# Three places instead of four for streamed weight blocks, one more block kept in SBUF

## Chip, cores, metric

One core of a Trainium2 chip. The metric is the device time of one execution in microseconds, as a median over runs; lower is better. In the texts and profile lines PE is the TensorE matmul engine (PEld its weight loads), DVE, ACT and POOL are VectorE, ScalarE and GpSimd, and SP is the engine whose queue issues the loads; SBUF and PSUM are the memories on the core.

## The reference, cut to what matters

The program does two independent things and joins the results: a state-space convolution B (2048 positions, 1024 channels), and a recurrent attention A in which each of 64 segments needs the memory rows that the segment before it has put out.

```python
for s in range(n_seg):                      # 64 segments of 32 rows, in series
    xs = x[:, s * seg_len:(s + 1) * seg_len, :].copy()
    h = jnp.concatenate([mem, xs], axis=1)
    q = jnp.einsum('btd,dhe->bhte', h, Wq)  # 1024 x 4096 each, bf16
    k = jnp.einsum('btd,dhe->bhte', h, Wk)
    v = jnp.einsum('btd,dhe->bhte', h, Wv)
    # ... masked softmax over 40 keys ...
    o = jnp.einsum('bhtk,bhke->bhte', p, v)
    o = jnp.einsum('bhte,hed->btd', o, Wo)  # 4096 x 1024
    mem = o[:, :M, :].copy()                # 8 rows for the next segment
```

(The index letters of the third product are shortened.) The weights are 64 blocks of 128 x 2048 bf16, 512 KB each, 32 MB together. They do not all fit into SBUF, and each segment needs all of them.

## The kernel before

Part B comes first and also prepares what part A needs: the streamed weight blocks are copied into DRAM tiles of their own (`WD`). Then the loop over the segments runs. A block is resident in SBUF, or kept in PSUM (two blocks), or streamed into one of four places, in turn:

```python
STREAM = {("k", 0): (0, 5), ("q", 0): (3,), ("k", 1): (0, 3), ("q", 1): (0, 4), ("v", 0): (0, 4), ("v", 1): (0, 4)}
STREAM_O = (0, 4, 8, 11, 13)
# ...
SLOTS = 4
# ...
    def unit(key):
        if key in rest:                       # first segment: a resident block comes in
            rest.remove(key)
            load_resident(tc, wres, src, key, W_res)
        if key in W_res:
            return W_res[key]
        if key in kept:
            return ahead_of.pop(key)
        between.pop(key, lambda: None)()      # small transfers hung in between
        t_ = wst.tile([128, 2048], BF16, name="wst", tag="w%d" % (loads[0] % SLOTS))
        loads[0] += 1
        nc.sync.dma_start(out=t_[:], in_=WD[key][:])
        return t_
# ...
            for kc in kcs:                    # one projection, 8 blocks
                w = unit((m, t, kc))
                for g in range(4):
                    for o_, rhs in columns(w, 512 * g, 512):
                        nc.tensor.matmul(a[32 * g:32 * g + 32, o_:o_ + rhs.shape[1]], lhsT=hT[:, kc, :], rhs=rhs,
                                         # ...
```

The place of a block is free again when PE has done its 4 matmuls (8 in the output product). SP then issues the next load into it; SP takes its instructions in program order. In part B, sums over residue classes of the input u ("class sums") run in the gaps of a loop of 17 rounds of 8 steps:

```python
            if e % 2 == 0 or (e == 7 and sb % 4 == 1):
                step_side()
```

## Time and profile before

| | before |
|---|---|
| median, 4 runs (2662.08 to 2674.72) | 2667.72 us |
| first segment's output in the profiled run | 925.0 us |
| distance of two segments' outputs, mean of 63 | 26.49 us |
| PE's waits for streamed blocks per segment | 3.46 us |
| DMA share and rate in the loop | 0.95, 335 GB/s |
| issue of a streamed load to its last engine's landing, median of 970 | 5.59 us |

The segment distance times 63 is 1669 of the 2655 us in the profile: a tenth of a microsecond per segment is 6.3 us. A place goes through a turn: PE frees it, SP issues, the load lands, PE uses it. With four places, the load of a streamed block cannot be issued before PE has finished the streamed block four earlier. The profile lines for these numbers stand in the prediction.

### The profile page before, as it was taken

To read this page: it belongs to the slowest core of one execution; us is meant where nothing else is said; L and a number is where in the kernel's file an instruction comes from. 1 tells how busy PE (TensorE), PEld (TensorE's weight loads), DVE (VectorE), ACT (ScalarE), POOL (GpSimd) and SP (SyncE) were. 2 spreads that over 40 slices of the span, in tenths; PEclk is the share of its full clock that TensorE was granted. 3 is DMA by queue.
4 is the path that set the end of the run, shared out by engine and by line. 5 is a ranking of instruction groups with operands and counts; after the bars stand their busy time and mean duration, and the time that the engine had idled before them with its cause. 6 is when DMAs were issued, how large, how long until landed. Compare 5 with 4: busy or idle time off the path is not lost.

```text
span 2655.4 us, 76588 instructions
## 1 busy us (share of the span) xinstructions
PE 2099.2 (79%) x32856; PEld 1120.4 (42%) x32902; DVE 1498.8 (56%) x3224; ACT 1022.6 (39%) x1550; POOL 311.7 (12%) x601
## 2 busy tenths in 40 slices
PE   1688788675978588888887887788888888888878
PEld 1365555532433244444444444444444444444444
DVE  9677777879882254445454545454545454454440
ACT  6888888831212132323232222222322323232221
POOL 2133433540001000000000000000000000000020
PEclk6799999888999698999999999999999999998899
DMA  5665854742339999999999999999999999999992
GB/s 138 173 192 161 247 165 137 189 125 87 116 127 333 334 335 328 330 349 329 344 334 347 339 334 322 332 331 335 340 332 339 339 337 338 344 332 321 317 352 88
DMA packets 373171, 729.62 MB, mean 275 GB/s; under 512 B 117654, under 2 KB 209782, under 8 KB 370782
## 3 DMA queue, kind: packets, MB, share of 16 engines
q1 hardware_dynamic: 354942, 671.08, 74.4%
q0 software_dynamic: 14128, 39.99, 4.4%
q10 hardware_dynamic: 3760, 13.65, 1.4%
q8 instruction: 257, 4.21, 0.6%
q14 instruction: 84, 0.69, 0.1%
HBM read 669.80 MB, written 67.36 MB: 278 GB/s over the span
## 4 chain that ended last, share of the span: by engine, by line
DMA 39%; PE 31%; DVE 10%; issue 8%; ACT 7%; POOL 1%; SPq 0%; ACTq 0%; POOLq 0%; DVEq 0%
PE acc L329 16%; DMA wst<-WD_o 16%; DMA wst<-WD_v 11%; DMA wst<-WD_k 7%; PE pp L428 3%; PE pe L551 2%; ACT sn L1019 2%; DMA wst<-WD_q 2%; PE pro L151 2%; ACT kM L994 1%; PE tr L340 1%; ACT E L991 1%; PE ups L850 1%; PE pro L138 1%; DVE nr L995 1%
## 5 line engine op out<-in xcount | busy, mean ns | idle before, releaser
L329 PEld LDWEIGHTS <-hT 128*32 128x32 bf16 x12352 | 344.8, 101 | 464.9 <-issue 222.2
L329 PE MATMUL acc<-wst,hT 128*32 128x512 bf16 x2816 | 302.3, 413 | 138.0 <-DMA wst<-WD_v 57.0
L335 ACT CAST ev<-acc 128x512 bf16<-128x512 f32 x384 | 224.8, 585 | 432.7 <-PE acc L329 428.3
L428 PEld LDWEIGHTS <-oT 128*32 128x32 bf16 x8192 | 209.7, 98 | 209.5 <-issue 182.4
L329 PE MATMUL acc<-W_q,hT 128*32 128x512 bf16 x3328 | 240.2, 394 | 0.0
L329 PE MATMUL acc<-W_k,hT 128*32 128x512 bf16 x2816 | 238.2, 442 | 0.0
L428 PE MATMUL pp<-wst,oT 128*32 128x256 bf16 x2560 | 132.7, 284 | 128.2 <-DMA wst<-WD_o 119.8
L268 DVE TENSOR_SCALAR piece<-keep 128x256 int32<-128x256 int32 (+1 forms) x640 | 189.3, 361 | 78.4 <-PE pp L428 58.2
L428 PE MATMUL pp<-W_o,oT 128*32 128x256 bf16 x5120 | 217.3, 280 | 6.6 <-DMA W_o<-in_A_Wo_dram 6.6
L329 PE MATMUL acc<-W_v,hT 128*32 128x512 bf16 x3072 | 216.0, 384 | 8.2 <-DMA W_v<-in_A_Wv_dram 8.2
L367 DVE TENSOR_REDUCE mx<-sc 128x8 f32<-128x320 f32 x128 | 62.6, 489 | 219.5 <-PE sc L360 219.4
L341 DVE COPY KT<-tr 128x512 bf16<-128x512 bf16 x64 | 27.1, 424 | 267.1 <-PE tr L340 267.1
L415 ACT CAST oT<-pv 128x512 bf16<-128x512 f32 x128 | 74.9, 585 | 195.5 <-PE pv L401 194.3
L1158 PE MATMUL yp<-Bt,mi 128*128 128x512 bf16 x379 | 112.8, 403 | 39.8 <-DMA mi<-MId 30.4
L348 POOL COPY KT<-pk 128x128 bf16<-128x128 bf16 x128 | 37.7, 294 | 882.9 <-PE acc L329 545.3
L341 ACT COPY QT<-tr 128x512 bf16<-128x512 bf16 x128 | 74.9, 585 | 166.3 <-PE tr L340 165.4
L518 ACT CAST ob<-pp 128x128 bf16<-128x128 f32 x64 | 17.0, 265 | 291.2 <-DVE ob L517 291.2
L995 DVE SCALAR_TENSOR_TENSOR nr<-kM,ptt 128x656 f32<-128x656 f32 x128 | 104.8, 831 | 42.8 <-ACT kM L994 42.6
L151 PE MATMUL pro<-xTl,wsl 128*128 128x512 bf16 x493 | 116.5, 384 | 13.0 <-DVE kst L155 7.7
L517 DVE CAST ob<-pp 128x128 bf16<-128x128 f32 x64 | 18.6, 291 | 181.4 <-PE pp L428 181.4
L302 POOL COPY hT<-xt 128x192 bf16<-128x192 bf16 x64 | 22.2, 347 | 760.2 <-DMA xt<-XTd 632.3
L369 ACT ACTIVATE sc<-sc 128x320 f32<-128x320 f32 x128 | 54.0, 422 | 147.5 <-DVE sc L368 143.6
(284 smaller groups left out, 3820.2 us busy)
## 6 DMA issues: line engine op xcount, KB each, us to landing
wst<-WD_o SPq DMA_DIRECT2D x320, 512.0 KB, 9.7
wst<-WD_k SPq DMA_DIRECT2D x256, 512.0 KB
wst<-WD_v SPq DMA_DIRECT2D x256, 512.0 KB, 5.9
wst<-WD_q SPq DMA_DIRECT2D x192, 512.0 KB, 4.7
Ud<-ux POOLq DMA_DIRECT2D x16, 1024.0 KB, 4.7
uq<-Ud SPq DMA_DIRECT2D x32, 512.0 KB, 7.5
pk<-PKd SPq DMA_DIRECT2D x64, 192.0 KB, 5.0
wsl<-in_A_Wk_dram SPq DMA_DIRECT2D x16, 512.0 KB, 4.5
```

Of the source, the lines that this page charges most:

```text
L151: nc.tensor.matmul(a[:], lhsT=w[:, kc, 128 * j:128 * j + 128], rhs=xTl[:, kc, :, :].rearrange("p s k -> p (s k)"), start=(kc == 0), stop=( ...
L268: nc.vector.tensor_scalar(out=out.bitcast(I32), in0=in_.bitcast(I32), scalar1=0, scalar2=None, op0=ALU.bitwise_or)
L329: nc.tensor.matmul(a[32 * g:32 * g + 32, o_:o_ + rhs.shape[1]], lhsT=hT[:, kc, :], rhs=rhs, start=(kc == 0), stop=(kc == KC - 1), tile_pos ...
L335: nc.scalar.copy(out=q[:], in_=a[:])
L341: eng(out=dst, in_=p[:, i, :, :, :])
L367: nc.vector.tensor_reduce(out=mx[:], in_=sc, axis=AX.X, op=ALU.max)
L369: nc.scalar.activation(out=sc, in_=sc, func=ACT.Exp, scale=scale)
L415: nc.scalar.copy(out=o[:], in_=p[:].rearrange("p a (g q) -> p a g q", g=4))
L428: nc.tensor.matmul(po[32 * qt:32 * qt + 32, :], lhsT=oT[:, h % 4, (h % 16) // 4, :], rhs=columns(w, 1024 * hh + 256 * qt, 256)[0][1], star ...
L551: nc.tensor.matmul(pe[n][:], lhsT=left[2 * b + hi // 16][:, 128 * (hi % 16):128 * (hi % 16) + 128], rhs=wo[u][:, 1024 * hh + 512 * n:1024 ...
L995: v.scalar_tensor_tensor(out=nrs[e // 4][:, e % 4].rearrange("p f t j -> p f (t j)"), in0=kM[:], scalar=MAGIC, in1=ptv, op0=ALU.subtract, ...
L1158: pe.matmul(yp[:], lhsT=m_[:, cs, kc, :], rhs=Bt[:, kc, half, j, c_, :], start=(n == 0), stop=(n == 15))
```

## The change

Intent: 4 KB per partition of SBUF go from the fourth place to one more resident block, so that a sixteenth less is streamed. Besides, the class sums start two steps later and end in the last round.

```diff
-STREAM_O = (0, 4, 8, 11, 13)
+STREAM_O = (0, 4, 8, 11)
...
-SLOTS = 4
+SLOTS = 3
...
-            if e % 2 == 0 or (e == 7 and sb % 4 == 1):
+            if (e % 2 == 0 and (sb or e)) or sb == 16:
                 step_side()
```

## The prediction

> **What bounds the kernel now.** I read the page first (busy shares, the slices over time, the queues), then the table of windows over the second part, then the chain of waits there, the table of waits, and last the timeline block by block. The program has two parts. Up to about 800 us it builds a convolution; from 868 us to 2594 us it walks 64 segments in series (63 distances of 26.5 us from the first to the last output copy, 925.0 to 2594.2 us). Each segment multiplies by 64 weight blocks of 512 KB: 46 stay in SBUF, two stay in PSUM, 16 are streamed anew through four places. The second part is two thirds of the span, so it decides. The page, then the window over 63 segments (PE, PEld, DVE, ACT, POOL, granted clock, DMA share, GB/s):
>
> ```profile
> DMA  5665854742339999999999999999999999999992
> q1 hardware_dynamic: 354942, 671.08, 74.4%
> 925.00:2594.20 1669.20, 1375.03 (x26838) 715.36 (x26840) 819.54 (x2269) 486.63 (x945) 70.35 (x203) 0.94 0.95 335
> ```
>
> The DMA engines look full (0.95), PE is busy 82%. A reader would conclude "DMA-bound: one block of 16 less is a sixteenth of the loop". The chain of waits says otherwise (start, us, what):
>
> ```profile
> 1407.29 5.24 DMA wst<-WD_v
> 1412.53 0.04 issue
> 1412.57 1.05 PE acc L329 x16
> ...
> 1415.78 5.79 DMA wst<-WD_o
> 1421.57 0.04 issue
> 1421.61 0.92 PE pp L428 x24
> ...
> 1424.52 5.63 DMA wst<-WD_k
> ```
>
> It alternates. A DMA piece starts when PE has finished with a place and SP issues the next load into it, and ends when that load lands. Its 5 to 6 us are four transfers' time, because three others stand before it; then PE work follows, then another such turn. So the loop is bound by turns of places woven with PE work, not by either alone. The sizes, over those 63 segments (total, times, longest):
>
> ```profile
> PE pp L428 <- DMA wst<-WD_o: 117.2, 149, 2.7
> PE acc L329 <- DMA wst<-WD_v: 56.3, 72, 2.1
> PE acc L329 <- DMA wst<-WD_k: 36.9, 44, 1.8
> PE acc L329 <- DMA wst<-WD_q: 7.4, 17, 1.1
> ```
>
> Their sum is 217.8 us, 3.46 us per segment. PE work, with its small waits for other engines, is the other 23 us.
>
> **What the Trainium skill says.** "DMA: Bandwidth & Descriptors", section "Why a DMA increments its semaphore by 16 and not by 1": a load is spread over up to 16 engines which finish independently, and only the full count says it has landed. The trace agrees: over 970 streamed blocks the 16 updates of one semaphore lie 1.86 us apart from first to last (median), the last comes 1.18 us after the middle one, and issue to last update is 5.59 us. So a block waits for its unluckiest engine, and a short queue leaves the lucky ones idle. Same page, "Anatomy of one DMA": about 2 us fixed beside bytes/436e9, stated for the GpSimd path. For 512 KB that gives 3.2 us; the trace's fastest undisturbed 512 KB load, of the spectra, issued by SP, took
>
> ```profile
> DMA to landing us min/median/max: 3.7/7.5/9.6
> ```
>
> 3.7 us. "HBM Reference", "Specifications (TRN2)": a core streaming alone gets about 425 GB/s. Here a 4 KB packet usually takes 159 ns on its engine, which over 16 engines is 412 GB/s; the mean is 183 ns, as one packet in fourteen takes over 200 ns. So 335 GB/s holds much waiting, and a DMA share of 0.95 is not the ceiling it looks.
>
> **The change, part by part.**
>
> (a) *One block less.* Wo block 13 becomes resident. It is still multiplied, so PE work is unchanged. Its 8-matmul group at 0.4 us is no longer waited for. Transfer per segment falls from 16 blocks at 128 packets x 183 ns / 16 engines = 1.46 us by one. If transfer alone were the bound, this would save 63 x 1.46 = 92 us.
>
> (b) *Three places.* I took from the timeline, for 56 segments, the distance from one streamed block's first matmul to the next one's, less the waits for DMA. In order of use (us): k0 1.62, k5 1.77, q3 1.57, k1:0 0.74, k1:3 2.10, q1:0 0.90, q1:4 1.36, v0:0 1.34, v0:4 1.75, v1:0 1.55, v1:4 1.25, o0 1.04, o4 2.18, o8 0.80, o11 0.63, o13 2.32; sum 22.92. A turn of four places costs 5.59 us (issue to landing) plus 0.47 us (matmuls on the block, SP's issue) = 6.06 us and brings PE four blocks on. Where four distances sum to less, the turn is longer and PE waits for the excess. The best set of turns that do not overlap: k1:0 to v0:0 (0.74+2.10+0.90+1.36 = 5.10, excess 0.96), v0:0 to o0 (5.89, 0.17), o0 to o13 (1.04+2.18+0.80+0.63 = 4.65, 1.41). Sum 2.54, so 25.46 us per segment. Measured is 26.4: scatter of the landings adds 0.9, as the longest of several random sums exceeds the sum of means.
>
> The same with three places. A turn has one transfer less before it, 5.59 - 1.46 = 4.13, but cannot go far below the undisturbed 3.7 us, and the trace shows the floor coming: where the earlier load's middle engine finished 2.75 us after this issue, this one's did 1.50 us later; with 1.75 us it was 1.92, with 1.25 us 2.01. Engines ran dry between. I add 0.3 for that: 4.43 + 0.47 = 4.9 us (estimate). Now o11's distance is 0.63+2.32 = 2.95. The best set: k5 to k1:3 (1.77+1.57+0.74 = 4.08, excess 0.82), q1:0 to v0:4 (0.90+1.36+1.34 = 3.60, 1.30), v0:4 to o0 (4.55, 0.35), o0 to o11 (4.02, 0.88). Sum 3.35, so 26.27; with the same 0.9 of scatter 27.2. Against 26.4 that is +0.8 us per segment, 63 x 0.8 = +51 us. So the lost place should cost more than the lost block gives. The waits for DMA should grow from 3.5 to 4.3 us per segment, while the DMA share falls to about 0.87 (bytes per segment 335 x 26.5 = 8.88 MB, less 0.52 MB; 0.95 x 8.36/8.88 x 26.5/27.2).
>
> (c) *First segment and end.* Resident and streamed loads together stay 36 in the first segment: about +2 us for the shorter queue. The final product has one block less to fetch, behind ten resident ones: nothing.
>
> (d) *Class sums later.* The order of instructions shows the same counts on PE and the sums moved back. At the start two exponent groups now come before the first sum (1.7 us in the chain). By the end of round 15 the side work has taken 63 steps instead of 68, so five sums run in round 16. The first falls into this hole of PE and is free:
>
> ```profile
> 552.32 0.25 PE L899 MATMUL kp<-cs 128*64 128x41 bf16 x2 [9.16 <-DVE cs L1027]
> ```
>
> The other four stand between the last groups of kernel products: 4 x 1.05 = 4.2 us, on the chain that releases the next stage. In return five sums leave earlier rounds, where ACT, DVE and PE alternate on the chain: about 0.8 us each (my estimate: half of the 1.05 us on PE, as about every second sum is in the chain, and half of an evacuation of 0.6 us), 4 us. Sum: 4.2 - 4 - 1.7 = -1.5 us, rounded to -2.
>
> Total: 51 + 2 - 2 = +51; 2671 + 51 = 2722 us, taken as 2723.
>
> **The rivals.** *Transfer bound:* the share 0.95 speaks for it; 63 x 1.46 = 92 us come back, about 2580 us. Against it: waits for DMA are only 3.46 us per segment, so even their end would give PE's 22.9 us, and the chain is half PE. A milder form, in which the slow packets come on all engines at once, makes the queue's depth matter little: waits then fall by up to 1 us, 2610 to 2650. The spread of 1.86 us within a block speaks against that. *Floor of the turn higher than I took:* if a turn of three costs 4.6 + 0.47 = 5.07 us, each of the four turns loses 0.17 more than I took, 63 x 0.68 = 43 us: 2766 us. The bend from 1.50 to 2.01 us speaks for this. *A new wait elsewhere:* SP issues in order, and the next segment's small load xt is now issued one release later; POOL's copy of it ended at 1629.75 us where DVE began the pieces of block 15 at 1629.68, so about a microsecond could come on the path at the segment's end. But the queue before it is one block shorter. That would be up to +30 us.
>
> **Range and chances.** The turn's length decides: 4.82 us in place of 4.9 gives +0.5 per segment (2703), 5.07 gives +1.5 (2766). I allow for the milder rival below and the new wait above: 2660 to 2785. Slower by over 2% begins at 2724, right at my value: nearly even between same and slower. Faster needs under 2617, thus nearly the pure transfer bound: 6%.
>
> **What would show each step.** Segment distance 27.2 us; waits of PE for streamed blocks about 4.3 us per segment; DMA share about 0.87 with GB/s near 305; issue to landing in the chain 4 to 5 us instead of 5 to 6, with four turns per segment; the first part within 4 us of before. I am wrong if the share stays at 0.95 with shorter segments (transfer bound), if PE's waits for streamed blocks fall, or if the first part moves by more than 10 us.

## The result, and the profile after

2849.78 us (median of 4, 2829.47 to 2859.03) against 2667.72: 6.7% slower, ratio 1.0671 with a 95% interval of 1.0605 to 1.0737. A ratio in this document is the mean time of one kernel's runs over the mean of the other's in the same rounds, so not quite the ratio of the medians. The edit leaves every block multiplied from its own tile.

The window over the 63 segments of the changed kernel, with the same columns as in the prediction:

```profile
940.20:2796.80 1856.60, 1390.86 (x26838) 719.80 (x26840) 824.91 (x2269) 486.86 (x945) 70.32 (x203) 0.94 0.85 284
```

The stretch is 1856.6 us instead of 1669.2: 29.47 us per segment, 2.98 more. PE's busy time and the granted clock are nearly the same, and the DMA share fell from 0.95 to 0.85. So no engine got more work; all of them stand still more. The waits of PE in that stretch (total, times, longest):

```profile
PE acc L329 <- DMA wst<-WD_k: 136.5, 119, 3.1
PE pp L428 <- DMA wst<-WD_o: 135.3, 164, 2.4
PE acc L329 <- DMA wst<-WD_v: 95.3, 116, 3.2
PE acc L329 <- DMA wst<-WD_q: 30.0, 43, 2.7
```

They sum to 397.1 us, 6.30 us per segment instead of 3.46. That is 2.84 of the 2.98 us. The chain of waits shows what such a wait is now:

```profile
1234.44 0.84 PE pp L428 x24
...
1236.56 0.43 PE pp L428 x8
1237.01 5.16 DMA wst<-WD_k
1242.17 0.04 issue
1242.21 0.87 PE acc L329 x10
1243.09 4.47 DMA wst<-WD_k
1247.60 0.40 PE acc L329 x4
...
1250.14 4.58 DMA wst<-WD_v
1254.76 1.07 PE acc L329 x16
1255.91 0.59 ACT ev L335
1256.50 0.04 issue
1256.55 0.42 PE acc L329 x4
1256.99 4.85 DMA wst<-WD_o
```

Four turns of 4.5 to 5.2 us in 25 us, with some 6 us of other work between them. This is one of the quicker stretches: over the whole loop the chain holds 3.7 such pieces per segment, 5.27 us each in the mean; in the kernel before it holds 2.5, of 5.97 us. One load in four-place streaming took 5 to 6 us; a load with one transfer less before it should have been 1.46 us quicker, and it is only some 0.7 us quicker. Over 816 streamed loads of this trace the median from issue to last landing is 4.87 us.

The first segment's output comes at 940.2 us instead of 925.0, so 15 us of the 202 us between the two profiled runs arise before the second segment.

### The profile page after: what moved, and what is told of

The parts are those of the page before. It is cut to its first block, busy times and chain, and to the rows that moved or that the text cites. A ratio compares the mean times of both kernels' runs of the same rounds, so it can differ in the third digit from the quotient of the medians.

```text
span 2857.3 us, 76451 instructions
## 1 busy us (share of the span) xinstructions
PE 2117.5 (74%) x32856; PEld 1124.8 (39%) x32902; DVE 1498.7 (52%) x3224; ACT 1023.9 (36%) x1550; POOL 306.9 (11%) x601
## 4 chain that ended last, share of the span: by engine, by line
DMA 46%; PE 26%; issue 8%; DVE 8%; ACT 7%; POOL 1%; SPq 1%; ACTq 0%; POOLq 0%; DVEq 0%
DMA wst<-WD_k 15%; DMA wst<-WD_o 14%; PE acc L329 12%; DMA wst<-WD_v 12%; PE pp L428 4%; DMA wst<-WD_q 3%; ACT sn L1020 2%; PE pe L551 2%; PE pro L151 1%; PE ups L850 1%; DVE nr L995 1%; ACT E L991 1%; PE tr L340 1%; ACT kM L994 1%; DVE m L1109 1%
## 5 line engine op out<-in xcount | busy, mean ns | idle before, releaser
L329 PE MATMUL acc<-W_v,hT 128*32 128x512 bf16 x3072 | 223.4, 394 | 9.2 <-DMA W_v<-in_A_Wv_dram 9.2
L329 PE MATMUL acc<-W_k,hT 128*32 128x512 bf16 x2816 | 226.1, 424 | 0.0
L428 PE MATMUL pp<-wst,oT 128*32 128x256 bf16 x2048 | 106.1, 283 | 143.1 <-DMA wst<-WD_o 137.3
L341 DVE COPY KT<-tr 128x512 bf16<-128x512 bf16 x64 | 27.2, 425 | 253.2 <-PE tr L340 253.2
L1075 PE MATMUL hps<-KT,MF 128*128 128x512 bf16 x374 | 95.3, 401 | 17.8 <-DVE x L1088 13.4
L994 ACT ACTIVATE kM<-ptt,magic 128x656 f32<-128x656 f32 x128 | 103.8, 811 | 7.1 <-PE ptt L931 7.1
```

The source lines that it names most:

```text
L341: eng(out=dst, in_=p[:, i, :, :, :])
L428: nc.tensor.matmul(po[32 * qt:32 * qt + 32, :], lhsT=oT[:, h % 4, (h % 16) // 4, :], rhs=columns(w, 1024 * hh + 256 * qt, 256)[0][1], star ...
L994: sc.activation(out=kM[:], in_=ptv, func=ACT.Identity, bias=magic[:])
L1075: pe.matmul(ps[:], lhsT=MF[:, 4 * rr + mc, cs, 128 * kc:128 * kc + 128], rhs=rhs, start=(i == 0 and mc == 0), stop=(i == 1 and mc == 3))
```

## The experiments

The theory to test: the time of the loop is made of turns, and a lost place costs more than a block less gives. Rivals: the loss sits in the added resident block or its addresses; in the class sums; or the loop is bound by bytes, and something else slowed the transfers. "Segment" is the mean distance of the segments' outputs in the profiled run, "landing" the median from issue to the last of a streamed load's 16 semaphore updates, "waits" PE's waits for streamed blocks per segment, "clock" the granted TensorE clock, both over the 63 segments.

| places / streamed | run | median us | ratio to before, 95% interval | segment | landing | waits | clock |
|---|---|---|---|---|---|---|---|
| 4 / 16 | before | 2667.7 | | 26.49 | 5.59 | 3.46 | 0.94 |
| 3 / 15 | changed kernel | 2849.8 | 1.0671 [1.0605, 1.0737] | 29.47 | 4.87 | 6.30 | 0.94 |
| 3 / 15 | loop alone | 2859.0 | 1.0679 [1.0626, 1.0731] | 29.47 | 4.89 | 6.20 | 0.94 |
| 4 / 16 | sums alone | 2679.2 | 1.0012 [0.9948, 1.0076] | 26.44 | | 3.26 | 0.93 |
| 3 / 16 | | 2958.4 | 1.1055 [1.0986, 1.1123] | 31.17 | 4.90 | 6.66 | 0.90 |
| 4 / 15 | wrong result | 2590.2 | 0.9675 [0.9625, 0.9726] | 25.40 | 5.65 | 3.40 | 0.99 |
| 1 / 16 | one look | 5238.0 | | 66.96 | 3.49 | 29.51 | 0.55 |
| 2 / 16 | one look | 3490.6 | | 39.61 | 4.31 | 12.96 | 0.84 |
| 5 / 16 | wrong result | 2591.3 | 0.9719 [0.9669, 0.9770] | 25.53 | 6.28 | 2.49 | 0.95 |
| 3 in halves / 15 | | 2793.3 | 1.0480 [1.0414, 1.0545] | 28.51 | | 4.09 | 0.96 |
| 4 in halves / 16 | | 2634.6 | 0.9894 [0.9844, 0.9943] | 26.24 | | 2.34 | 0.95 |
| 3 / 15, other blocks | | 2794.3 | 1.0493 [1.0447, 1.0539] | 28.46 | 4.85 | 5.22 | 0.95 |
| 5 / 17 | | 2647.3 | 0.9944 [0.9896, 0.9992] | 26.29 | 6.27 | 2.97 | 0.96 |
| 1 / 16, half loads | one look, wrong result | 4394.2 | | 53.84 | 2.58 | 19.51 | 0.63 |

The check does not notice a block multiplied from another block's data; that the other kernels are correct follows from their edits, which leave every block its own weights.

### Each part by itself

The loop's part alone (the changed kernel with the old line for the class sums):

```diff
-            if (e % 2 == 0 and (sb or e)) or sb == 16:
+            if e % 2 == 0 or (e == 7 and sb % 4 == 1):
```

> Three places and 15 streamed blocks, class sums where they were before. If the loop carries the loss (my theory: the turn of three places came out at 4.87 us issue to landing instead of the 4.43 us I took): within 15 us of the changed kernel, about 2840 us, segment distance 29.4 us. If the later class sums carry a real part of it (rival): 15 us or more below the changed kernel.

Measured: 2858.99 us (2850.5 to 2865.1), within 10 us of the changed kernel's median, and 29.47 us per segment as there. The loop carries the whole loss, as far as the noise lets one see.

The class sums alone (the kernel before with the new line):

```diff
-            if e % 2 == 0 or (e == 7 and sb % 4 == 1):
+            if (e % 2 == 0 and (sb or e)) or sb == 16:
```

> The kernel before with the class sums a quarter round later and nothing else. My prediction's step (d) said -2 us. The trace of the changed kernel shows its first segment's output 15 us later than before; if the sums do that, this run is 10 to 15 us slower than before (about 2680 us); if the three places do it (fewer loads in flight while the resident blocks come in), it is within 4 us of before.

Measured: the same time as before, 1.0012, within 0.65% or 17 us. The traces show a loss rather than a gain. The first spectrum product with a negated kernel (`hps<-KN,MF` in the traces) starts at 579.3 to 580.5 us in all four profiled kernels that have the later sums, and at 569.5 to 575.1 us in the ten without them. That is about 7 us at this point; the times are too coarse to confirm it at the end.

The place alone (the kernel before, `SLOTS = 3`):

```diff
-SLOTS = 4
+SLOTS = 3
```

> Three places, still 16 streamed blocks; 4 KB per partition stay unused. Theory of turns: the worst of all, since the lost place costs in each turn and no block is given back: turns of 5.34 us against the measured distances give about 29.5 us without scatter, 30.4 with 0.9 of scatter, so 2670 + 63 x 3.9 = about 2915 us. Rival (the loss comes from the added resident block, its place in SBUF or the changed addresses, not from the number of places): about 2670 us.

Measured: 2958.4 us, the slowest of the three-place kernels with whole blocks, as the theory of turns says, and some 40 us above its number. The rival (added block, addresses) falls: nothing was added here, and the loss is even larger. PE's busy time in the loop also rose, at a lower granted clock:

```profile
931.10:2894.60 1963.50, 1462.31 (x26839) 744.49 (x26840) 823.59 (x2268) 487.60 (x945) 70.66 (x203) 0.90 0.88 285
```

Of the 4.67 us more per segment, 3.20 are waits for streamed blocks. The other 1.47, some 93 us in all, are PE's own time, at a granted clock of 0.90 against 0.94 before. The 40 us may be part of that; no run separates it.

The block alone. With four places there is no SBUF for it, so it borrows the tile of block 12, and the result is wrong:

```diff
-STREAM_O = (0, 4, 8, 11, 13)
+STREAM_O = (0, 4, 8, 11)
...
     def unit(key):
+        if key == ("o", 13):
+            key = ("o", 12)
```

(Block 13 is also taken off the list of resident blocks.)

> Wrong result on purpose: four places, 15 streamed blocks, block 13 of Wo is multiplied from block 12's tile, so no SBUF and no transfer is needed for it. Theory of turns: the best sum of turns falls from 25.46 to 24.78 us per segment, so -0.7 x 63 = -43 us, about 2625 us. Transfer bound (rival): a block of 1.46 us less per segment, -92 us, about 2578 us. If the added block is what hurts: no faster than before.

Measured: 2590.23 us, 88 us less than before (2678.27 in these rounds). As a number this is nearer to the transfer bound's -92 than to my -43. In the profiled run the segment is 1.09 us shorter, 69 us over 63. But its trace does not show the gain where either reading puts it, in the waits. The window and PE's waits for streamed blocks (this kernel's lines stand two lower):

```profile
935.40:2535.70 1600.30, 1311.50 (x26839) 696.01 (x26840) 818.59 (x2269) 487.35 (x945) 70.72 (x203) 0.99 0.94 329
PE acc L331 <- DMA wst<-WD_k: 79.7, 89, 2.0
PE pp L430 <- DMA wst<-WD_o: 75.6, 105, 2.8
PE acc L331 <- DMA wst<-WD_v: 45.3, 49, 2.2
PE acc L331 <- DMA wst<-WD_q: 13.4, 22, 1.6
```

The waits sum to 214.0 us, against 217.8 before: they hardly fell. What fell is PE's busy time, by 63.5 us, at a granted clock of 0.99 against 0.94. All four timed runs share it: their mean clock over the whole program is 0.939 to 0.954, that of the seven runs of the kernel before in these rounds 0.911 to 0.928. Whether the missing load brings the clock, or the clock came by itself, no run separates. Nor do equal waits prove that the block saved none: with the same turn, a faster PE would by itself wait longer.

The two terms of the change, from the medians of this batch: the block gives 2678.3 - 2590.2 = 88 us, and the place, with 15 streamed, costs 2859.0 - 2590.2 = 269 us. With 16 streamed it costs 2958.4 - 2678.3 = 280 us. Both terms hold differences of the clock. In waits alone, the place costs 2.80 us per segment with 15 streamed and 3.20 with 16 (176 and 202 us in all), and the block gives 0.06 us at four places and 0.46 at three. That a place outweighs a block holds either way.

### The turn by itself

With one place, no load ever stands behind another.

```diff
-SLOTS = 4
+SLOTS = 1
```

> A measurement of the turn by itself: one place, 16 streamed blocks, so no load ever stands behind another and issue to landing is the fixed part plus one transfer. Floor theory (a load alone needs about as long as the 3.7 us seen for the spectra, so few places leave the DMA engines idle): 3.5 to 3.9 us from issue to landing, 16 x 4.2 = 67 us per segment, about 5200 us in all, DMA share near 0.35. Queue theory (a turn is just as many transfers of 1.46 us as there are places, with a small fixed part): issue to landing about 2 us, 16 x 2.5 = 40 us per segment, about 3500 us.

Measured: 5237.99 us, 66.96 us per segment; the floor theory had 5200 and 67. The chain of waits is now a plain alternation:

```profile
2001.41 3.59 DMA wst<-WD_o
2005.00 0.04 issue
2005.04 0.64 PE pp L428 x8
2005.68 0.02 issue
2005.70 3.53 DMA wst<-WD_o
2009.23 0.04 issue
2009.27 0.64 PE pp L428 x8
```

A load alone takes 3.5 us, and PE 0.64 us at a low clock. The window from 1000 to 2500 us of this run:

```profile
1000.00:2500.00 1500.00, 796.96 (x9566) 348.60 (x9562) 297.02 (x806) 174.31 (x335) 21.19 (x68) 0.55 0.42 132
```

The granted clock is 0.55 there, and PE idles between short bursts. The Trainium skill, "TensorE: Matmul & The Clock Gate", section "Part 1: The HAM clock gate", says that the clock is halved by default and released by activity; the 0.55 of this run fits that, though no run here isolates the rule.

Two places:

```diff
-SLOTS = 4
+SLOTS = 2
```

> Second point of the same curve: two places, 16 streamed blocks. Floor theory: issue to landing 4.1 us (only 0.4 us more than alone, as the second load hides in the first one's fixed part), turn 4.6 us per two blocks, 37 us per segment, about 3350 us. Queue theory: 2.9 us, turn 3.4 us, 28 us per segment, about 2770 us.

Measured: 3490.64 us, landing 4.31 us. The floor theory is nearer (3350 us, 4.1 us) than the queue theory (2770 us, 2.9 us).

Five places, 16 streamed; the SBUF comes from multiplying block 14 of Wo from block 12's tile (wrong result):

```diff
-SLOTS = 4
+SLOTS = 5
...
     def unit(key):
+        if key == ("o", 14):
+            key = ("o", 12)
```

> The other direction: five places, 16 streamed blocks; wrong result on purpose (block 14 of Wo is multiplied from block 12's tile, which gives the SBUF for the fifth place). Floor theory with a turn of 6.7 + 0.47 = 7.2 us per five blocks: the best sum of turns against the measured distances is under 24.7 us, but 16 transfers of 1.46 us and the small ones need 25.1 us, so the transfers now bind: about 25.4 us per segment, -65 us against the kernel before. If four places had already been enough (transfer bound): no change.

Measured: 2591.32 us, 77 us less than before in its rounds (2667.98), 25.53 us per segment against the expected 25.4. The window over its 63 segments:

```profile
920.50:2528.70 1608.20, 1357.24 (x26839) 710.42 (x26840) 816.84 (x2268) 486.99 (x945) 70.29 (x203) 0.95 0.97 348
```

The share of the DMA engines rises by only 0.02 over the kernel before, but the rate by 13 GB/s: the "full" 0.95 had held room. Here is the main result. Landing with 1, 2, 3, 4 and 5 places and 16 streamed blocks is 3.49, 4.31, 4.90, 5.59 and 6.28 us. A further place lengthens the turn by 0.6 to 0.8 us and not by a transfer's 1.46 us, so a turn divided by its places falls steadily: with 0.47 us for PE and SP it is 3.96, 2.39, 1.79, 1.52 and 1.35 us per block.

Why 0.7 and not 1.46? At the moment of an issue, the load before it has, on its middle engine (the ninth of the 16 to finish), a median of 2.81 us still to go with four places and 1.99 us with three (changed kernel). What stands before a load is 0.82 us shorter, not 1.46. The queue was not short of loads: in 86% and 89% of the issues none of the loads in the other places had fully landed. Why the rest shrinks by so little, no run separates. And of the 0.82 us a part is lost again: from the middle engine of the load before to that of this load it takes 1.59 us in the one kernel and 1.91 us in the other. So from issue to the middle engine it is 4.39 and 3.84 us, only 0.55 less.

What a load without others is made of: one place and half loads of 256 KB, each half used twice (wrong result).

```diff
-        t_ = wst.tile([128, 2048], BF16, name="wst", tag="w%d" % (loads[0] % SLOTS))
+        t_ = wst.tile([128, 1024], BF16, name="wst", tag="w%d" % (loads[0] % SLOTS))
         loads[0] += 1
-        nc.sync.dma_start(out=t_[:], in_=WD[key][:])
-        return t_
+        nc.sync.dma_start(out=t_[:], in_=WD[key][:, 0:1024])
+        return [(0, 1024, t_), (1024, 1024, t_)]
```

(with `SLOTS = 1`; the two blocks kept in PSUM are loaded through tiles of their own)

> One place and loads of half a block (256 KB, 2 KB per partition), each half used twice: wrong result on purpose. It splits the undisturbed turn into a fixed part and a part by size. One place with whole blocks took 3.49 us from issue to landing (median). If 0.64 us of transfer time is all that depends on size, 2.85 us here and a fixed part of 2.2 us; if slow packets make it longer, 2.5 us and a fixed part of 1.5 us. Segment about 57 us, total near 4600 us.

Measured: 2.58 us, against 3.49 with whole blocks. The difference of 0.91 us for 256 KB lies between the two numbers that I had given, nearer to the second. So a lone load is about 1.67 us that do not depend on size and 1.82 us that do (an estimate from these two sizes; the rows differ too, 2 and 4 KB). The total of 4394 us is below the expected 4600.

### Undoing the loss in other ways

Halves. Three places of 512 KB become six of 256 KB; a half is freed after two matmuls instead of four, and PE starts when the first half has landed.

```diff
-        t_ = wst.tile([128, 2048], BF16, name="wst", tag="w%d" % (loads[0] % SLOTS))
-        loads[0] += 1
-        nc.sync.dma_start(out=t_[:], in_=WD[key][:])
-        return t_
+        halves = []
+        for n in range(2):
+            t_ = wst.tile([128, 1024], BF16, name="wst", tag="w%d" % (loads[0] % HALVES))
+            loads[0] += 1
+            nc.sync.dma_start(out=t_[:], in_=WD[key][n])
+            halves.append((1024 * n, 1024, t_))
+        return halves
```

(`HALVES = 6` on the changed kernel; the DRAM copies are laid out by halves.)

> The changed kernel with its three places cut into six halves of 256 KB, each loaded and freed by itself; correct result, same SBUF, twice the number of loads. Theory of turns: a half is asked for again 0.2 us earlier and PE begins on a block when its first half has landed, so a turn is 0.3 to 0.5 us shorter: 27.6 to 26.8 us per segment without scatter, 0.4 to 1.2 less than 28.0, about 2775 to 2825 us. Rival (a fixed cost for each load binds, SP or the DMA rings): slower than the changed kernel.

Measured: 2793.26 us, inside the range of the theory of turns. PE's waits fell by 2.21 us per segment, but its other time rose by 1.25 us; why, no run shows. The same on the kernel before, `HALVES = 8`:

> The kernel before with its four places cut into eight halves of 256 KB, correct result, same SBUF. Six halves gained 57 us on three places. Theory of turns: 0.3 to 0.5 us less per turn, three turns per segment, 0.75 to 1.1 us per segment, but 16 transfers at 1.43 us and the small ones need about 25 us, so at most 1 us is to be had: 2610 to 2640 us. If four places are bound by transfers alone: no change, 2670.

Measured: 2634.59 us, 1.1% under the kernel before (0.9894, interval 0.9844 to 0.9943), correct. Of all correct kernels here it has the lowest median. Here too PE's waits fell more, by 1.12 us per segment, than the segment did (0.25).

Other blocks. The changed kernel with three places, but streaming blocks that lie evenly along PE's work:

```diff
-STREAM = {("k", 0): (0, 5), ("q", 0): (3,), ("k", 1): (0, 3), ("q", 1): (0, 4), ("v", 0): (0, 4), ("v", 1): (0, 4)}
-STREAM_O = (0, 4, 8, 11)
+STREAM = {("k", 0): (0, 4), ("q", 0): (1, 7), ("k", 1): (4,), ("q", 1): (0, 6), ("v", 0): (2, 6), ("v", 1): (0, 4)}
+STREAM_O = (0, 6, 8, 14)
```

(The small transfers are hung before the blocks k0:4, k1:4 and o8.)

> The changed kernel (three places, 15 streamed) with other blocks streamed, so that PE's distances from one to the next are even: 1.25 to 2.08 us instead of 0.74 to 2.95. Correct result, same bytes, same number of loads. Theory of turns: three places at 5.34 us per turn give 26.7 us per segment at best against 28.0 with the old set, so up to 1.3 us less, 2770 to 2815 us. If the loss came from the bytes or from the DMA engines' rate alone, the set would not matter: 2850 us.

Measured: 2794.28 us, 28.46 us per segment, 1.0 less than the changed kernel with the same places, the same bytes, the same number of loads and the same landing (4.85 us). PE's waits fell by 1.08 us per segment at nearly the same clock. That the set matters at all is what a bound by bytes cannot give, and what turns woven with PE's distances must give. The small transfers moved with the set; that they are what matters is untested.

The change turned round: five places, 17 streamed.

```diff
-... ("k", 1): (0, 3), ...
+... ("k", 1): (0, 3, 6), ...
-SLOTS = 4
+SLOTS = 5
```

> The change turned round: five places, 17 streamed blocks (block 6 of the second K tile added), correct result, same SBUF as before. Turns of 6.28 + 0.47 = 6.75 us per five blocks bind at 17/5 x 6.75 = 23 to 24 us per segment; transfers need 17 x 1.43 + 1.5 = 25.8 us. So the transfers bind: about 26.0 us against 26.5, 2640 to 2660 us. If one place is worth as little as I took in my prediction (a turn shortened by 1.46 us per place): 2720 us or more.

Measured: 2647.29 us, ratio 0.9944 (0.9896 to 0.9992). A block more is streamed, and the time is not longer, if anything 0.6% shorter. Its segment of 26.29 us is near the 26.0 that the transfers' bound gave.

## Why the prediction was wrong

The direction and the mechanism were right: the loop is bound by turns of places woven with PE's work, and the lost place costs more than the block gives. The size was wrong, +182 us instead of +55 and beyond the upper end of the range (2785 us), mostly because of one term. The direction was a lean: the prediction called "same" and "slower" nearly even.

**What bounds the kernel: right.** The two parts of the change measured apart (-88 and +269 us; in waits about 4 and 176 us), the curve over one to five places, and the run with other blocks show it. The reading that a DMA share of 0.95 is no ceiling was right: five places move 348 GB/s against 335. One reading beside it was off: the chain is not "half PE"; over the 63 segments of the kernel before, DMA pieces are 57% of it and PE 37%.

**(a) One block less: the number fits, the reason is not shown.** 1.46 us of transfer were to be worth at most 92 us; at four places the block gave 88 us in time, 69 us by the segments of the profiled run. My sum of turns left 0.68 us per segment (43 us) of it, as shorter waits. The waits fell by 0.06 us only, and PE's own time by 1.03 us, at the higher granted clock. So 88 being close to 92 is no support for a bound by transfers, and may be luck; what the block is worth at an equal clock stays open.

**(b) Three places: the step that failed.** I wrote "A turn has one transfer less before it, 5.59 - 1.46 = 4.13", and then added 0.3 for the floor: 4.43 us from issue to landing. The run has 4.87. The reading behind it fails with it: the 5 to 6 us of a turn are not "four transfers' time", for a load with none before it takes 3.49 us, and each further place adds 0.6 to 0.8 us. Put 4.87 into the same sum (4.87 + 0.47 = 5.34 us per turn): the four turns' excesses become 1.26, 1.74, 0.79 and 1.32 us, 5.11 instead of 3.35, so 28.03 us per segment, 28.9 with the 0.9 of scatter, against 27.2 predicted and 29.47 measured. The 0.44 us in one turn, times four turns, is 1.76 us of the 2.27 that were missing, or 111 of the 143 us. The other half microsecond is in part 0.13 us more of PE's own time (segment less waits, 23.17 us instead of 23.04); for the rest the scatter may be larger than 0.9, which had been fitted to 26.4 where 26.49 was measured; no run splits that further. The clue was in my own text: with 1.25 us to go for the load before, this load's middle engine was done 2.01 us after that one's, half a microsecond more than 1.50. I used it as a correction of 0.3 us on a subtraction that was too large to begin with. What a place is worth in a turn has to be taken from the queue that really stands before a load (0.82 us shorter) and from the time that is lost again when it is short, not from a full queue's one transfer.

**(c)** was given as +2 us and was not measured apart. The first output of the loop-alone run came at 931.4 us against 925.0, in single profiles; without the later sums and with four or five places it came at 920.5 to 935.4, so they scatter by more.

**(d) Class sums: -2 us predicted, no change measured in the time** (1.0012, within 17 us). In the traces the spectrum products start about 7 us later, in four profiles against ten, so the sign was wrong as well; which of its terms failed was not traced.

**The rivals.** The transfer bound (2580 us) and its milder form failed. "Floor of the turn higher than I took", with 2766 us, was the right one and still too small: its turn was to be 5.07 us, and it is 5.34. (The 3.2 us that the prediction works out from the skill's formula is an estimate for another path; the lone load takes 3.49 us.) The new wait at xt was not found in the chain. SP's in-order issue did put a small store on the chain in places (1.74 us at 1209.57 us in the changed kernel); no run isolates what that costs over the whole loop.

**What would show each step:** DMA share 0.87 predicted, 0.85 measured, with 284 GB/s instead of 305; four turns per segment predicted, 3.7 pieces per segment in the chain; issue to landing in the chain 4 to 5 us predicted, 5.27 in the mean there; waits 4.3 us predicted, 6.30 measured; segment 27.2 predicted, 29.47 measured; first part within 4 us predicted, 15 us later measured. That is beyond the 10 us that the prediction had named as a sign of being wrong; it is 15 of the 182 us or so, about half of it the class sums.

Open: why four-KB packets are slow more often with few places (mean 183 ns with four places, 194 in the changed kernel, 205 with one), and whether the granted clocks of the 3/16 run (0.90) and of the 4/15 run (0.99) are cause or effect.

## What to carry to other kernels

Where PE and a ring of buffers alternate, list the distances of the consumer between streamed blocks and the turn (free, issue, land, use), and look for the stretches in which a ring's worth of distances is shorter than the turn. Before a buffer is traded for fewer bytes, measure the turn at several depths: here a place was worth 269 us and a block 88, while the DMA share of 0.95 suggested the opposite. Look at the waits and the granted clock beside the time: the block's 88 us came with a higher clock and hardly shorter waits. If SBUF is short, finer pieces of the same buffer (halves, -1.1% on the kernel before) or an even spacing of the streamed blocks (-1.0 us per segment at three places) buy back part of a place at no SBUF.

## What the Trainium skill lacked or had wrong

- "DMA: Bandwidth & Descriptors", "Anatomy of one DMA", has about 2.0 us fixed plus bytes/436e9, for the GpSimd path. For loads issued by SP, alone on the engines, this case has 2.58 us for 256 KB and 3.49 us for 512 KB: about 1.67 us fixed and 0.91 us per 256 KB, 288 GB/s by that difference instead of 436 (an estimate from two sizes, one look each, with rows of 4 and 2 KB).
- No page says how issue to landing grows with the loads in flight, which decides how many buffers a stream needs. Here 3.49, 4.31, 4.90, 5.59 and 6.28 us for 1 to 5 places of 512 KB, at DMA shares of 0.42, 0.72, 0.87, 0.95 and 0.97 and 132, 224, 285, 335 and 348 GB/s.
- The same page says under "Why a DMA increments its semaphore by 16 and not by 1" that the engines finish independently, but not by how much: 1.86 us from first to last with four places, 0.58 us with one (medians).
- "Perfetto Trace Analysis", "Identifying the Most-Contended Engine", warns that the occupancy of 16 DMA engines misleads. From a share of 0.95 to 0.97 the rate rose from 335 to 348 GB/s and the time fell by 2.8% (ratio 0.9719). Share and rate need not even rank alike: four places in halves had 0.98 with 339 GB/s, five places with 17 blocks 0.97 with 358.
